# Two-stage attention and soft mixture of experts on one core: later stores in row halves on SyncE's queue, 28 zero products in front, one zero product fewer near the end

## The chip, the cores and the metric

The kernel runs on one core of a Trainium2 chip. The metric is device time in microseconds (us) for one launch. The core has a matrix engine (TensorE, in the profile PE, its weight loads PEld), a vector engine (VectorE, DVE), a scalar engine (ScalarE, ACT), a general engine (GpSimd, POOL) and a control engine (SyncE, SP). Transfers between the chip's memory (HBM) and the core's memory run on 16 DMA engines; they are issued here from POOL's queue and from SP's queue. Matrix products end in PSUM, from where DVE or ACT move them ("evict" them) to the core's main memory.

## The reference

There are two steps. The first is causal attention for 4 batches, 8 heads, 768 positions and head size 64; three of the heads see all earlier positions, the other five only the first 4 positions and a window of 64. The second is a soft mixture of experts on the 3072 rows of 512 that attention gives.

```python
scores = scale * np.matmul(q, k.transpose(0, 1, 3, 2))
scores = np.where(mask, scores, -1e9)          # causal; or causal & (first 4 | last 64)
a = softmax(scores); attn = np.matmul(a, v)    # -> x: (3072, 512)

logits = x @ phi                               # (3072, 32): 8 experts of 4 slots
d = softmax(logits, axis=0); slot_input = d.T @ x
for e in range(8):
    slot_out[e] = np.maximum(slot_input[e] @ w1[e], 0.0) @ w2[e]   # 512 -> 1024 -> 512
c = softmax(logits, axis=1)
out = c @ slot_out                             # (3072, 512) float32
```

## The kernel before

**Order of the work.** The kernel is written as a list of named steps, each with the engines that may do it, an assumed cost, a key (about the time at which it is due) and the steps and buffers that it needs. A planner in the file (`Plan.run`) simulates the engines and fixes one order per engine; that order is the program. Every engine then works through its own list and waits on semaphores for the others. The planner counts PE's instructions with the number `mm` that a step states, not with what its function emits.

**Attention.** A batch is worked in four pairs of heads. PE transposes the loaded rows of q, k and v (lines L604 for the first batch, L630 for the others, eviction by the helper lines L334 and L336), forms the scores (L656), ACT takes the exponential (L726), DVE multiplies by the mask (L672), PE multiplies by v (L800), DVE divides (L824), and PE transposes the result for the logits (L836).

**The front.** POOL issues the loads of the first batch and writes small index tables; the last of these is `unit` (L419). SP issues three transfers (L475 to L477): half of the first expert matrix, the flags of the heads, and phi. DVE sets `zt`, a tile of zeros (L499). PE's first step is `TD` (two products, L427 and L428), which needs the tables; then come the transposes of phi (L528), the flag product (L513), a second group for phi (L536), and the transposes of the first batch (L604). Between these stand five zero products of 448 columns (`ZG`, L505), which the planner places and whose results nobody reads.

**The mixture of experts.** The expert matrices come in fp32 and are cast to bf16 on the way in, all from POOL's queue. Of w1 and w2 most come as one transfer of 1 MB (as written); the last two matrices of w2 (numbers 14 and 15, the tiles pt and qk) come in two column halves of 256, in the order 14 left, 15 left, 14 right, 15 right, so that the left half of `slot_out` is ready before the right half has landed. After the products with w1 (L1008) and w2 (L1046) ACT scales a half of `slot_out` (L1104).

**The output.** It is 24 tiles of 128 rows by 512 columns: six groups `gi` of four tiles `r`, where the four tiles of a group hold interleaved rows. Groups 0, 1 and 2 are made in two column halves: all twelve left halves as soon as the left half of `slot_out` is there, then all twelve right halves; groups 3, 4 and 5 are then made whole. One output product is L1121, its eviction with the division by the row sum L1131 (DVE) or L1129 (ACT), in turns. The stores (L1140) are:

- left, from POOL's queue: group 0 as tile 0 and tiles 1 to 3; group 1; group 2 (four transfers);
- right, from SP's queue: group 0 as tiles 0 and 1, tiles 2 and 3; group 1; group 2 (four transfers);
- whole groups 3, 4 and 5, from SP's queue (three transfers of 1 MB).

Three zero products of 448 columns (`ZT0`, `ZT1`, L1064) stand in PE's list ahead of the last w2 matrix of each column half:

```python
for c in range(2):
    for e in range(NE - NSPLIT, NE):
        w2_op(e, c, c + 1)
        if e == NE - 2:
            wait_zeros(f"ZT{c}", 3, kt + (29.5 + e if c else 22.5), w2o[c], c == 0)
```

The store step, which the change calls with other rows and another queue:

```python
def store(eng, m, gi, r0, r1, cs, key):
    def emit_st(o):
        dst = out[512 * gi:512 * (gi + 1), :].rearrange("(p r) d -> p r d", r=4)
        (nc.gpsimd if eng == "POOL" else nc.sync).dma_start(dst[:, r0:r1, cs], ot_view(gi)[:, r0:r1, cs])
```

Of the kernel before, what the change touches and what calls it, by code (L numbers as in the profile page):

```python
# [151 lines left out]
def pe(ns, n=1):  # L152
    occ = ns * n / 1000.0
    return {"PE": (occ, occ + 0.27)}
# [72 lines left out]
def kernel(  # L227
# [13 lines left out]
    nc = tc.nc  # L241
    P = 128
    B, H, S, D = q.shape
# [37 lines left out]
    zt = sb.tile([P, 448], BF16, name="zt")  # L281
# [16 lines left out]
    tq, krow, unit = xr[:, 0:256], xr[:, 256:384], xr[:, 384:640]  # L298
    jrow = xT.rearrange("p a c -> p (a c)")[:, 1536:1792].bitcast(F32)
    td = xT.rearrange("p a c -> p (a c)")[:, 640:1152].bitcast(F32)  # L300
    rne, frow = xr[:, 1792:1824].bitcast(F32), xr[:, 1824:1832]
# [4 lines left out]
    trb = [ps.tile([P, 512], F32, name=f"tr{i}") for i in range(2)]  # L306
    pvb = ps.tile([P, 2, 512], F32, name="pv")

    def tr_bf(s, n):
        return trb[s].bitcast(BF16)[:, 0:n]  # L310
# [10 lines left out]
    pl = Plan({"S8": 11, "QT": 2, "KT": 2, "VT": 1, "VB": 2, "VF": 3, "PT": 2, "PTX": 2, "XB": 2,  # L321
               "XT": 1, "SC": 2, "TR": 2, "PV": 1, "BK": 8})
# [6 lines left out]
    def on(eng, occ, late=0.18):  # L329
        return {eng: (occ, occ + late)}  # L330
# [50 lines left out]
    def w_mem(i):  # L381

        m = late_mem[i]() if i in late_mem else slots[wbuf[i].slot][:, :]
        return m.rearrange("p (h x) -> p h x", h=2)[:, :, 0:4 * KB]
# [37 lines left out]
    def head_const(o):  # L422
        nc.vector.tensor_scalar(ident, jrow, pc[:, 0:1], None, op0=ALU.is_equal)

    def emit_td(o):
        t = trb[tdb.slot][:, 0:256]
        nc.tensor.matmul(t, unit[:, 0:128], tq, start=True, stop=False)  # L427
        nc.tensor.matmul(t, krow, unit, start=False, stop=True)  # L428

    def key_pos(o):  # L430
        t = trb[tdb.slot][:, 0:256]
        nc.vector.tensor_scalar(pc[:, 2:3], t[:, 0:1], -float(n_sink), None, op0=ALU.is_gt)
        nc.vector.tensor_copy(td, t)
        nc.vector.scalar_tensor_tensor(edist[:, 0:256], td, -30000.0, td, op0=ALU.mult, op1=ALU.max)
        nc.vector.tensor_copy(edist[:, 256:768].rearrange("p (a c) -> p a c", a=2),
                              edist[:, 0:256].rearrange("p (o c) -> p o c", o=1).to_broadcast([P, 2, 256]))
# [11 lines left out]
    def head_flags(o, n):  # L448
        cp = nc.scalar.copy if o.eng == "ACT" else nc.gpsimd.tensor_copy
        for a, j0, j1 in ((1, 1, 4), (0, 0, 1)):  # L450
            cp(fmx[:, n, :, j0:j1, :].rearrange("p i j d -> p i (j d)"),
               thr[:, a, n::4].rearrange("p (i o) -> p i o", o=1).to_broadcast([P, 2, 66 * (j1 - j0)]))
# [54 lines left out]
    for x in range(5):  # L507
        o_z = pl.op(f"ZG{x}", pe(372), 60.0, deps=[o_z], lead=9.6 + 1.2 * x, emit=emit_zg, mode="full", mm=1)
    o_kp = pl.op("key_pos", on("DVE", 1.2), -79, deps=[o_td], rel=[tdb], emit=key_pos)
    flb = Buf("TR")  # L510
    o_fr = pl.op("flag row", on("DVE", 0.2), -10, deps=[o_sp], emit=flag_row)
    o_fp = pl.op("flag product", on("PE", 0.07, 0.27), -10, deps=[o_fr, o_tab], acq=[flb], mode="r32", mm=1,
                 emit=lambda o: nc.tensor.matmul(trb[flb.slot][:, 0:H], unit[:, 0:128], frow, start=True, stop=True))  # L513
    o_fl = pl.op("flags", on("DVE", 0.45), -10, deps=[o_fp, o_kp], rel=[flb], emit=flags)
    o_fm, o_hm = {}, {}
    for n in range(4):
        o_fm[n] = pl.op(f"fm{n}", on("ACT", 0.65) if n == 0 else on("POOL", 0.9), -8 if n == 0 else T * n - 3.5,
                        deps=[o_fl], emit=lambda o, n=n: head_flags(o, n))
# [15 lines left out]
    def phi_t2(o):  # L534
        for n in range(4):
# [8 lines left out]
                  emit=lambda o: nc.vector.tensor_copy(  # L544
                      phi4, tr_bf(pb2.slot, 4 * NS).rearrange("p (n r s) -> p n r s", n=4, r=1).to_broadcast(
                          [P, 4, 4, NS])))
# [3 lines left out]
    def load_tile(ti):  # L550

        tbuf[ti], tland[ti], p0 = Buf("S8"), [], 0
        for x, b, x0, x1 in TILES[ti]:
# [8 lines left out]
                  emit=lambda o, x=x: nc.gpsimd.tensor_copy(w_mem(0)[:, 0, KB * x:KB * (x + 1)],  # L562
                                                            w0f[:, KB * x:KB * (x + 1)])) for x in range(4)]
# [82 lines left out]
    def evs(x, b, n):  # L646
        return ev[x, 0, n // 2] if b == 0 else [e for x0, x1, e in ev[x, b] if x0 < 6 * n + 6 and x1 > 6 * n]
# [32 lines left out]
    for b in range(B):  # L680
        for n in range(4):
# [5 lines left out]
            def emit_v2(o, n=n, tr=tr):  # L687
                t = tr_bf(tr.slot, 768)
                for j in range(6):
# [3 lines left out]
                      emit=emit_v2, mode="full", mm=6)  # L693

            def emit_vb(o, b=b, n=n, tr=tr):
# [4 lines left out]
                           acq=[VBb[b]] if n == 0 else [], rel=[tr], emit=emit_vb)  # L700
            VFb[p] = Buf("VF")

            def emit_vf(o, b=b, n=n, p=p):
# [4 lines left out]
                           emit=emit_vf)  # L708

            PTb[b, n] = Buf("PT")  # L710
            for kk, g in enumerate(range(5)):
# [3 lines left out]
                def emit_qk(o, b=b, n=n, g=g, sc=sc):  # L715
                    parts, c = [], 0
                    for j, q0, nb in PGROUPS[g]:
# [5 lines left out]
                          acq=[sc], rel=[QTb[b], KTb[b]], emit=emit_qk, mode="r64", mm=2 * len(PGROUPS[g]))  # L723

                def emit_ex(o, b=b, n=n, g=g, sc=sc):
# [4 lines left out]
                                   acq=[PTb[b, n]] if kk == 0 else [], rel=[sc], emit=emit_ex)  # L730
                for m, gs in enumerate(MGROUPS):
                    if gs[-1] == g:
                        o_m = pl.op(f"MK.{p}.{m}", on("DVE", [0.605, 0.605, 0.335][m]), key + 0.3,
                                    deps=[expo[p, x] for x in gs] + [o_hm[n]], emit=mask_emit(b, n, m))
# [3 lines left out]
        for ns in ([(0, 1), (2, 3)] if b == 0 else [(0, 1, 2, 3)]):  # L738
            sc = Buf("SC")

            def emit_lx(o, b=b, sc=sc, ns=ns):
# [4 lines left out]
                      deps=list(dict.fromkeys(e for n in ns for x in "qk" for e in evs(x, b, n))),  # L746
                      acq=[sc], rel=[QTb[b], KTb[b]], emit=emit_lx, mode="r64", mm=2 * len(ns))

            def emit_ex2(o, b=b, sc=sc, ns=ns):
# [4 lines left out]
            e = pl.op(f"EXX.{b}.{ns[0]}", on("ACT", 0.12 + 0.213 * len(ns)), key - 1.0, deps=[a, PTXb[b].op],  # L754
                      acq=[PTXb[b]] if ns[0] == 0 else [], rel=[sc], emit=emit_ex2)

            def emit_mx(o, b=b, ns=ns):
# [4 lines left out]
            e = pl.op(f"MX.{b}.{ns[0]}", on("DVE", 0.07 + 0.134 * len(ns)), key + 0.3, deps=[e] + [o_hm[n] for n in ns],  # L762
                      emit=emit_mx)
# [5 lines left out]
    for b in range(B):  # L769
        for n in range(4):  # L770
# [9 lines left out]
            for i in iorder:  # L780
                deps, need = [v2e[p], vfo[p]] + [o_z][p:], set()
# [7 lines left out]
                def emit_pv(o, b=b, n=n, p=p, i=i, pv_at=pv_at):  # L789
                    pT = pTs[PTb[b, n].slot]  # L790
                    vb = vbs[VBb[b].slot]
                    for h in range(2):
                        bk, c = pv_at(h, i)
                        for j in range(i + 1):
# [3 lines left out]
                            else:  # L798
# [5 lines left out]
                             deps=list(dict.fromkeys(deps)) + ([last] if last else []),  # L804
                             acq=[PVb[p]] if i == 0 else [],
# [7 lines left out]
            for i0, i1 in halves:  # L813
                part = f"{p}" if i1 - i0 == 6 else f"{p}.{i0}"

                def emit_nm(o, i0=i0, i1=i1, b=b, n=n, p=p):
# [3 lines left out]
                    else:  # L820
# [8 lines left out]
                                 deps=[pvo[i1 - 1], XBb[b].op], acq=[XBb[b]] if n == 0 else [], rel=[PVb[p]],  # L829
                                 emit=emit_nm)  # L830

                def emit_xt(o, i0=i0, i1=i1, b=b, n=n, tr=tr):
                    t = tr_bf(tr.slot, 768)
                    xv = xbs[XBb[b].slot]
                    for i in range(i0, i1):
# [3 lines left out]
                          acq=[tr] if i0 == 0 else [], rel=[XBb[b]], emit=emit_xt, mode="full", mm=i1 - i0)  # L839

                def emit_xe(o, i0=i0, i1=i1, n=n, tr=tr):
# [4 lines left out]
                               acq=[XTb[b]] if n == 0 else [], rel=[tr], emit=emit_xe)  # L846
# [9 lines left out]
        if b < B - 1:  # L856
            es = []
            for c in range(2):
                lg = Buf("TR")

                def emit_ls(o, c=c, lg=lg):
                    for n in range(4):
# [4 lines left out]
                          acq=[lg], rel=[XTb[b]], emit=emit_ls, mode="full", mm=4)  # L867
# [8 lines left out]
            def emit_tt(o, te=te):  # L876
                for i in range(6):
# [5 lines left out]
                           emit=lambda o, te=te: copy(o, elg.rearrange("p i s -> p (i s)"), tr_bf(te.slot, 6 * NS)))  # L883
# [8 lines left out]
        else:  # L892
            lg = Buf("TR")
            a = pl.op(f"LGa.{b}", pe(25, 18), kb - 6.0, deps=[xto[4 * b + n] for n in range(3)] + [o_phi],
                      acq=[lg], emit=lambda o, lg=lg, f=emit_lg: f(o, lg, ns=(0, 1, 2)), mode="full", mm=18)
            for i0 in (0, 3):
                a = pl.op(f"LG.{b}" if i0 else f"LGb.{b}", pe(25, 3), kb - 6.0, deps=[a, xhalf[i0]], rel=[XTb[b]],
                          emit=lambda o, lg=lg, f=emit_lg, i0=i0: f(o, lg, ns=(3,), i0=i0, i1=i0 + 3), mode="full", mm=3)
# [74 lines left out]
    kt = T * 16 + 10  # L973
# [7 lines left out]
    def emit_si(o):  # L981
        t = trb[si.slot][:, 0:4 * NS].rearrange("p (a s) -> p a s", a=4)
        sv = slot_sc.rearrange("p (di do) -> p do di", do=4)
        for do in range(4):
# [4 lines left out]
                  emit=lambda o: nc.vector.tensor_copy(siT.rearrange("p a s -> p (a s)"), trb[si.slot][:, 0:4 * NS]))  # L989
    zs, zb = [], Buf("SC")  # L990
    named = {o.name: o for o in pl.ops}
    for z, (name, n) in enumerate((("PV.15.5", 1), ("XT.15.3", 1), ("LG.3", 1), ("DS.3", 1), ("SI", 1))):
        def emit_z(o, n=n):
            for _ in range(n):
# [3 lines left out]
                        acq=[zb] if z == 0 else [], emit=emit_z, mode="full", mm=n))  # L998
    hse, hte = {}, {}
    for e4 in range(2):  # L1000
        hse[e4] = []
        for c in range(2):
            hp = Buf("BK")

            def emit_h(o, e4=e4, c=c, hp=hp):
                for do in range(4):
                    for g in range(4):
# [5 lines left out]
                      acq=[hp], emit=emit_h, mode="c32", mm=16)  # L1013
# [25 lines left out]
    w2o = {}  # L1039
# [21 lines left out]
    def wait_zeros(name, n, key, dep, first=False):  # L1061
        def emit_z(o):
            for _ in range(n):
                nc.tensor.matmul(banks[zw.slot][:, 0:448], ident, zt, start=True, stop=True)  # L1064

        pl.op(name, pe(190, n), key, deps=[dep], acq=[zw] if first else [], rel=[zw], emit=emit_z, mode="full", mm=n)
# [4 lines left out]
    for c in range(2):  # L1071
        for e in range(NE - NSPLIT, NE):
            w2_op(e, c, c + 1)
            if e == NE - 2:
                wait_zeros(f"ZT{c}", 3, kt + (29.5 + e if c else 22.5), w2o[c], c == 0)

    def out_lhs(gi, r):
        return expT[:, r, 128 * gi:128 * (gi + 1)]
# [2 lines left out]
    for x, (g0, g1) in enumerate(((0, 3), (3, 6))):  # L1081
# [8 lines left out]
        def emit_rr(o, g0=g0, g1=g1, rw=rw):  # L1090
# [4 lines left out]
                  acq=[rw], rel=[], emit=emit_rw, mode="full", mm=4 * (g1 - g0))  # L1095
# [4 lines left out]
    for c in range(2):  # L1100
        def emit_so(o, c=c):
# [3 lines left out]
            else:  # L1105
# [3 lines left out]
                          emit=emit_so))  # L1109
# [27 lines left out]
# [5 lines that stand above are left out]
        pl.op(f"ST.{m}.{gi}.{r0}", on(eng, 0.7), key, deps=[oe[m, gi, r] for r in range(r0, r1)], emit=emit_st)  # L1142

    NL = 12
    halved = [(gi, min(4, NL - 4 * gi)) for gi in range((NL + 3) // 4)]
    for gi, n in halved:
        for r in range(n):
            out_tile("l", gi, r, 0, 1, kt + 30 + 0.1 * (4 * gi + r))
    for gi, r0, r1 in [(0, 0, 1), (0, 1, 4)] + [(gi, 0, n) for gi, n in halved[1:]]:
        store("POOL", "l", gi, r0, r1, slice(0, 256), kt + 31 + gi + 0.1 * r0)  # L1150
    for gi, n in halved:
        for r in range(n):
            out_tile("r", gi, r, 1, 2, kt + 40 + 0.1 * (4 * gi + r))
        for r0, r1 in [(0, 2), (2, 4)] if gi == 0 else [(0, n)]:
            store("SP", "r", gi, r0, r1, slice(256, 512), kt + 41 + gi + 0.1 * r0)
    for gi in range(6):
        n = dict(halved).get(gi, 0)
# [55 lines left out]
```

## Time and profile before

| what | value |
|---|---|
| median of 3 runs | 148.62 us (148.15 to 148.8) |
| the profiled execution's own time | 148.91 us |
| its span, first to last instruction | 147.1 us |
| mean granted clock of TensorE | 0.968 |
| busy: PE, DVE, ACT, POOL | 119.7, 111.0, 107.9, 42.0 us |

The profile is of one execution on the chip. A row of the timeline gives the start and the length in us, the engine, the line of the kernel, the operation, what it writes and reads, its shape, how often it stands in that row, and in brackets the idle time before it and what ended that. A row of the chain of waits gives start, length and what the last chain of work was doing. The rows of transfers give their kind, their number, the size of each in KB, and the median time from issue to landing. "DMA share" is the mean busy share of the 16 DMA engines; it can exceed 1 where an engine has more than one packet under way.

### The profile page before, as it was taken

The page shows a single profiled execution, that of the slowest core. Times are in us where ns is not written, and L with a number is a line of the kernel's source. Part 1 is how long each engine was busy: PE and PEld are TensorE (multiplying, and loading weights), DVE is VectorE, ACT ScalarE, POOL GpSimd, SP SyncE. Part 2 cuts the span into 40 slices and gives each one's busy share as a digit, 9 for nine tenths or more (in the row PEclk, how much of TensorE's full clock was granted, in tenths as well). Part 3 has the DMA queues.
Part 4 walks back from the last instruction along what each step waited for, and adds up shares of the span by engine and source line. Part 5 has one row for each costly group of instructions (what it writes and reads, how often), then busy time and mean ns, then how long its engine had stood idle before and what let it go on. Part 6 is the DMA issues. An engine that isn't in the chain of part 4 may idle for free.

```text
span 147.1 us, 4879 instructions
## 1 busy us (share of the span) xinstructions
PE 119.7 (81%) x2107; PEld 79.2 (54%) x2107; DVE 111.0 (75%) x254; ACT 107.9 (73%) x147; POOL 42.0 (29%) x75
## 2 busy tenths in 40 slices
PE   0167988999989999999999999999959899879000
PEld 0045666677776657776558766666745445443000
DVE  1786299999999999999799899999973312549500
ACT  3152689999999997999998999999971460649200
POOL 6988631120311380100170011405380000340000
PEclk9999999999999999999999999999995999999965
DMA  5999999999999999999999999999999999989995
GB/s 147 270 207 212 217 213 214 213 215 211 216 215 214 212 215 214 217 214 214 215 215 217 214 215 214 214 214 215 214 214 214 206 196 197 168 309 347 404 423 212
DMA packets 13815, 33.40 MB, mean 227 GB/s; under 512 B 802, under 2 KB 6562, under 8 KB 13282
## 3 DMA queue, kind: packets, MB, share of 16 engines
q0 software_dynamic: 11472, 27.27, 94.1%
q1 hardware_dynamic: 2322, 5.83, 10.5%
q8 instruction: 16, 0.26, 0.6%
q14 instruction: 5, 0.04, 0.1%
HBM read 52.49 MB, written 6.29 MB: 400 GB/s over the span
## 4 chain that ended last, share of the span: by engine, by line
PE 27%; DVE 26%; DMA 18%; ACT 15%; issue 5%; POOL 1%; SPq 0%; DVEq 0%; ACTq 0%; POOLq 0%
DMA qk<-in_moe_w_dram 14%; ACT pt L726 11%; PE sc L656 6%; DVE pt L672 5%; PE pv L800 5%; DVE xv L824 5%; DMA phf<-in_moe_phi_dram 4%; DVE qk L336 4%; PE tr L604 3%; PE tr L630 3%; PE bk L1121 2%; PE tr L863 2%; DVE xv L336 2%; DVE slot L1131 2%; DVE vf L705 2%
## 5 line engine op out<-in xcount | busy, mean ns | idle before, releaser
L726 ACT ACTIVATE pt<-sc 128x1024 bf16<-128x1024 f32 x80 | 77.0, 1047 | 3.0 <-PE sc L656 2.8
L656 PE MATMUL sc<-qk 64*128 64x512 bf16 (+3 forms) x256 | 31.4, 311 | 1.2 <-ACT pt L726 0.8
L672 DVE TENSOR_TENSOR pt<-pt,msk 128x1024 bf16<-128x1024 bf16 (+1 forms) x48 | 29.0, 610 | 2.0 <-ACT pt L726 1.8
L800 PEld LDWEIGHTS <-pt 128*128 128x128 bf16 x640 | 23.4, 98 | 6.2 <-issue 5.2
L800 PE MATMUL pv<-vx,pt 128*128 128x65 bf16 x320 | 25.6, 193 | 0.3 <-DVE xv L824 0.2
L800 PE MATMUL pv<-vf,pt 128*128 128x65 bf16 x320 | 21.3, 195 | 0.9 <-DVE xv L824 0.9
L347 POOL DMA_DIRECT2D slot<-in_moe_w_dram x11 | 7.7, 696 | 40.0 <-PE tr L630 34.3
L336 DVE COPY qk<-tr 128x768 bf16<-128x768 bf16 (+2 forms) x33 | 15.1, 482 | 2.1 <-PE tr L604 1.8
L630 PE MATMUL tr<-ident,slot 128*64 128x128 bf16 (+1 forms) x448 | 16.3, 219 | 0.4 <-ACT qk L334 0.3
L824 DVE TENSOR_TENSOR xv<-pv,rs 128x768 bf16<-128x768 f32 (+1 forms) x17 | 15.5, 911 | 0.6
L630 PEld LDWEIGHTS <-slot 128*64 128x64 bf16 (+1 forms) x448 | 13.1, 109 | 5.1 <-issue 4.8
L656 PEld LDWEIGHTS <-qk 64*128 64x128 bf16 x256 | 10.4, 94 | 9.6 <-issue 3.3
L887 POOL COPY expT<-eT 128x192 bf16<-128x192 bf16 x12 | 7.4, 667 | 12.5 <-ACT eT L870 12.5
L1131 DVE TENSOR_SCALAR slot<-bk,rrow 128x256 f32<-128x256 f32 (+1 forms) x19 | 9.2, 562 | 2.2 <-PE bk L1121 2.2
L336 DVE COPY xv<-tr 128x512 bf16<-128x512 bf16 (+2 forms) x20 | 8.0, 410 | 2.5 <-PE tr L604 2.2
L836 PE MATMUL tr<-ident,xv 128*128 128x128 bf16 x96 | 8.4, 224 | 1.3 <-DVE xv L824 0.9
L604 PEld LDWEIGHTS <-slot 96*64 96x64 bf16 x192 | 6.8, 141 | 4.3 <-issue 4.0
L604 PE MATMUL tr<-ident_u,slot 96*64 96x96 bf16 x192 | 7.9, 248 | 1.6 <-DVE phi L544 1.1
L336 DVE COPY xT<-tr 128x768 bf16<-128x768 bf16 (+1 forms) x14 | 7.5, 539 | 1.1 <-PE tr L836 1.1
L1129 ACT ACTIVATE slot<-bk,rrow 128x256 f32<-128x256 f32 (+1 forms) x17 | 7.7, 570 | 0.9 <-PE bk L1121 0.9
L690 PE MATMUL tr<-ident,xv 128*128 128x128 bf16 x96 | 8.1, 220 | 0.0
L1140 POOL DMA_DIRECT2D out_dram<-slot x4 | 2.9, 714 | 17.7 <-DVE slot L1131 17.6
(121 smaller groups left out, 165.6 us busy)
## 6 DMA issues: line engine op xcount, KB each, us to landing
slot<-in_moe_w_dram POOLq DMA_DIRECT2D x10, 1024.0 KB, 24.6
out_dram<-slot SPq DMA_DIRECT2D x3, 1024.0 KB, 5.9
slot<-in_q_dram POOLq DMA_DIRECT2D x2, 768.0 KB, 19.9
slot<-in_k_dram POOLq DMA_DIRECT2D x2, 768.0 KB, 23.8
qk<-in_moe_w_dram SPq DMA_DIRECT2D x1, 1024.0 KB, 6.3
slot<-in_v_dram POOLq DMA_DIRECT2D x2, 512.0 KB, 21.5
qk<-in_moe_w_dram POOLq DMA_DIRECT2D x1, 1024.0 KB, 17.4
vx<-in_moe_w_dram POOLq DMA_DIRECT2D x1, 1024.0 KB, 21.5
```

Source lines behind the costliest of these rows:

```text
L336: nc.vector.tensor_copy(dst, src)
L347: acq=[buf] if buf else [], lead=1.3, emit=lambda o: nc.gpsimd.dma_start(dst(), src))
L604: nc.tensor.transpose(t[64 * i:64 * (i + 1), :, :, s, :], rv[:, i, 8 * c + s, :], ident_u)
L630: nc.tensor.transpose(t[64 * i:64 * (i + 1), :, s, :], rv[:, i, 8 * c + s, :], ident[0:R, 0:R])
L656: nc.tensor.matmul(scb[sc.slot][:, i, c:c + 128 * nb], kk, qq.rearrange("p b c -> p (b c)"), start=True, stop=True)
L672: nc.vector.tensor_tensor(pT, pT, mh, op=ALU.mult)
L690: nc.tensor.transpose(t[:, 128 * j:128 * (j + 1)], vT[:, 6 * n + j, :], ident)
L726: nc.scalar.activation(pTs[PTb[b, n].slot][:, :, 512 * g:512 * (g + 1)], scb[sc.slot], ACT.Exp, scale=scale)
L800: nc.tensor.matmul(pvb[:, bk, c:c + 65], lt, rhs, start=(j == 0), stop=(j == i))
L824: nc.vector.tensor_tensor(xo, pvw[:, :, :, 0:64], r.rearrange("p i (j o) -> p i j o", o=1).to_broadcast([P, 2, i1 - i0, 64]), op=ALU.mult)
L836: nc.tensor.transpose(t[:, 128 * i:128 * (i + 1)], xv[:, i, 128 * n:128 * (n + 1)], ident)
L1131: nc.vector.tensor_scalar(d, banks[bf.slot][:, 0:w], sc_, None, op0=ALU.mult)
```

## The change

Three edits.

1. In front, 28 zero products of 256 columns enter PE's list: 15 ahead of TD, 10 behind it, 3 behind the flag product. They write a part of PSUM that nobody reads before it is written anew. The planner's counts are not changed, so all other steps keep their order on every engine.
2. `ZT1`, ahead of the last w2 matrix of the right half, has two zero products instead of three.
3. The left stores of groups 1 and 2 go from POOL's queue to SP's, each in two transfers (tiles 0 and 1, tiles 2 and 3); on SP's queue they stand ahead of the right stores. The right stores of groups 1 and 2 are split in the same way. With the three transfers of the front, SP's queue then carries sixteen.

```diff
+    def fill(n):
+        for _ in range(n):
+            nc.tensor.matmul(pvb[:, 1, 0:256], zt[:, 0:128], zt[:, 0:256], start=True, stop=True)
+
     def emit_td(o):
+        fill(15)
         t = trb[tdb.slot][:, 0:256]
         nc.tensor.matmul(t, unit[:, 0:128], tq, start=True, stop=False)
         nc.tensor.matmul(t, krow, unit, start=False, stop=True)
+        fill(10)
...
-    o_fp = pl.op("flag product", on("PE", 0.07, 0.27), -10, deps=[o_fr, o_tab], acq=[flb], mode="r32", mm=1,
-                 emit=lambda o: nc.tensor.matmul(trb[flb.slot][:, 0:H], unit[:, 0:128], frow, start=True, stop=True))
+    def emit_fp(o):
+        nc.tensor.matmul(trb[flb.slot][:, 0:H], unit[:, 0:128], frow, start=True, stop=True)
+        fill(3)
+
+    o_fp = pl.op("flag product", on("PE", 0.07, 0.27), -10, deps=[o_fr, o_tab], acq=[flb], mode="r32", mm=1, emit=emit_fp)
...
-                wait_zeros(f"ZT{c}", 3, kt + (29.5 + e if c else 22.5), w2o[c], c == 0)
+                wait_zeros(f"ZT{c}", 2 if c else 3, kt + (29.5 + e if c else 22.5), w2o[c], c == 0)
...
-    for gi, r0, r1 in [(0, 0, 1), (0, 1, 4)] + [(gi, 0, n) for gi, n in halved[1:]]:
-        store("POOL", "l", gi, r0, r1, slice(0, 256), kt + 31 + gi + 0.1 * r0)
+    for gi, r0, r1 in [(0, 0, 1), (0, 1, 4)] + [(gi, x, x + 2) for gi, n in halved[1:] for x in (0, 2)]:
+        store("SP" if gi else "POOL", "l", gi, r0, r1, slice(0, 256), kt + 31 + gi + 0.1 * r0)
...
-        for r0, r1 in [(0, 2), (2, 4)] if gi == 0 else [(0, n)]:
+        for r0, r1 in [(0, 2), (2, 4)]:
             store("SP", "r", gi, r0, r1, slice(256, 512), kt + 41 + gi + 0.1 * r0)
```

## The prediction

> **What bounds the kernel now.** I read the page first, then the chain of waits, then the timeline of the last 20 us and the busy shares by stretch, and last the timeline of the first 16 us.
>
> ```profile
> span 147.1 us, 4879 instructions
> ...
> DMA  5999999999999999999999999999999999989995
> ...
> q8 instruction: 16, 0.26, 0.6%
> ...
> HBM read 52.49 MB, written 6.29 MB: 400 GB/s over the span
> ```
>
> The DMA engines are full in nearly every slice. What they carry is seen by stretch (columns: stretch, length, busy time of PE, PEld, DVE, ACT, POOL, granted clock, DMA share, GB/s):
>
> ```profile
> 0.00:1.70 1.70, 0.00 (x0) 0.00 (x0) 0.24 (x1) 0.97 (x1) 0.57 (x5) 1.00 0.00 0
> 1.70:2.70 1.00, 0.00 (x0) 0.00 (x0) 0.00 (x0) 0.31 (x1) 1.00 (x2) 1.00 0.95 205
> 30.00:105.00 75.00, 73.09 (x1407) 50.99 (x1404) 71.95 (x156) 72.39 (x92) 17.50 (x27) 1.00 1.06 214
> 110.00:115.00 5.00, 4.52 (x67) 2.92 (x66) 1.31 (x4) 1.35 (x3) 0.00 (x0) 0.66 1.05 211
> 127.00:131.00 4.00, 3.03 (x38) 1.41 (x37) 2.07 (x7) 2.41 (x7) 2.85 (x4) 1.00 0.79 203
> 132.00:145.00 13.00, 3.91 (x18) 1.44 (x15) 6.21 (x12) 4.94 (x11) 0.00 (x0) 0.85 1.03 397
> 134.00:137.00 3.00, 1.94 (x8) 0.58 (x6) 3.00 (x6) 2.94 (x6) 0.00 (x0) 1.00 1.05 368
> 137.00:145.00 8.00, 0.00 (x0) 0.00 (x0) 1.21 (x2) 0.00 (x0) 0.00 (x0) 0.75 1.03 422
> 145.00:147.10 2.10, 0.00 (x0) 0.00 (x0) 0.00 (x0) 0.00 (x0) 0.00 (x0) 0.50 0.10 39
> ```
>
> Two stretches are full: the loads (share 1.06 at 30 to 105 us) and the stores (1.03 at 132 to 145). Between them, at 127 to 131, the share falls to 0.79. The chain and the issue-to-landing table say what hangs on that seam:
>
> ```profile
> 107.20 0.09 POOL qk L347
> ...
> 108.94 21.16 DMA qk<-in_moe_w_dram
> 130.15 0.43 PE bk L1046 x8
> 130.59 0.48 ACT msk L1104
> ```
>
> ```profile
> qk<-in_moe_w_dram POOLq DMA_DIRECT2D x2, 512.0 KB, 19.4
> ...
> out_dram<-slot SPq DMA_DIRECT2D x2, 256.0 KB, 2.8
> ```
>
> The last half of the last w2 matrix (w15, in qk) is issued at 108.94 and lands at 130.1, because 21 us of other loads are queued ahead of it. From its landing everything right of column 256 follows in a row:
>
> ```profile
> 125.31 0.40 PE L1046 MATMUL bk<-qk,xT 128*32 128x256 bf16 x8
> ...
> 126.59 2.44 DVE L1131 TENSOR_SCALAR slot<-bk,rrow 128x256 f32<-128x256 f32 x6 [1.96 <-PE bk L1121]
> 126.70 2.30 ACT L1129 ACTIVATE slot<-bk,rrow 128x256 f32<-128x256 f32 x6 [0.47 <-PE bk L1121]
> ...
> 127.37 2.96 POOL L1140 DMA_DIRECT2D out_dram<-slot  x4 [17.56 <-DVE slot L1131]
> ...
> 128.56 0.74 PE L1064 MATMUL bk<-zt,ident 128*128 128x448 bf16 x3
> ...
> 130.15 0.40 PE L1046 MATMUL bk<-qk,xT 128*32 128x256 bf16 x8 [0.84 <-DMA qk<-in_moe_w_dram]
> ...
> 132.09 0.97 SPq L1140 DMA_DIRECT2D out_dram<-slot  x2
> ```
>
> PE idles 0.84 us for that load at 130.15; the first right-hand store leaves SP at 132.09, 1.94 us after the landing. So the time is: landing (130.15), 1.94 us of compute, and then stores at the full rate until 145.2. After 132.0 the engines move 13.0 x 397 + 2.1 x 39 KB = 5.24 MB of the 6.29 MB of output. The right halves (12 tiles of 128x256 f32, 1.57 MB) and the twelve full tiles (3.15 MB) make 4.72 MB, so 0.52 MB of left-hand output is still unsent when the right-hand stores begin. At the 368 GB/s of 134 to 137, where the runs are 1 KB, that is 1.4 us: the left stores end at about 133.4.
>
> **The zero products in front.** These rows carry their cost:
>
> ```profile
> 0.85 0.24 DVE L499 MEMSET zt<- 128x224 uint32 x1 [0.85 <-PEq L1194]
> ...
> 4.55 0.39 PE L427 MATMUL tr<-xT 1*128 1x256 bf16 x1 [4.55 <-POOL xT L419]
> 4.73 0.42 PE L428 MATMUL tr<-xT 1*128 1x256 bf16 x1
> ...
> 8.01 0.61 PE L528 MATMUL tr<-ident,phi 128*32 128x128 bf16 x4 [2.86 <-DVE xT L439]
> 8.55 0.18 PE L513 MATMUL tr<-xT 1*128 1x8 bf16 x1
> 9.28 0.28 PE L536 MATMUL tr<-ident,slot_acc 32*128 32x32 bf16 x4 [0.55 <-ACT slot_acc L334]
> ...
> 11.92 1.49 PE L604 MATMUL tr<-ident_u,slot 96*64 96x96 bf16 x32 [1.09 <-DVE phi L544]
> 13.34 0.93 PE L505 MATMUL pv<-zt 128*128 128x448 bf16 x2
> 14.20 1.49 PE L604 MATMUL tr<-ident_u,slot 96*64 96x96 bf16 x32
> 15.62 0.55 PE L505 MATMUL pv<-zt 128*128 128x448 bf16 x1
> ...
> 115.04 0.35 PE L995 MATMUL sc<-zt,ident 128*128 128x448 bf16 x1
> ```
>
> Two zero products of 448 columns take 0.93 us at 13.34 and one takes 0.55, so each further one costs 0.38. At the end three take 0.74 and one 0.35: 0.195 each. PE is at half speed in front, although the clock column shows 1.00 there. Scaled to 256 columns, a product costs 0.22 us in front and 0.11 at full speed. The first fifteen can start when zt is set (1.09) and end at 1.1 + 15 x 0.22 = 4.4 us; PE waits for POOL until 4.55 anyway, so they cost nothing (if zt came 0.5 us later, TD would be 0.35 us late). The ten behind TD run from 5.15 to 7.35 at most and PE waits for DVE until 8.01: nothing. The three behind the flag product run from 8.73 to 9.06 or 9.39, and the next product waits for ACT until 9.28: 0 to 0.1 us.
>
> What they bring is clock. The four groups at 11.92, 13.34, 14.20 and 15.62 alone are 4.46 us at half speed, so up to 2.2 us leave PE's front; since PE alternates there with landings and evictions I put the earlier start of attention at 1 to 1.5 us. The Trainium skill's "TensorE: Matmul & The Clock Gate", section "Part 1: The HAM clock gate", has full clock after a busy window of about 3.4 us and half clock after an idle one; the halved prices of the zero products agree, and by it the fillers release the clock before the transposes.
>
> Where does that 1 to 1.5 us go? Attention is engine-bound (PE, DVE, ACT 96 to 97% busy at 30 to 105 us), so it ends that much earlier. But the load that gates the right half is not: the DMA share is already 1.06 throughout and the last load is 21 us deep in its queue. I count 0 on the end. Only the left half can start sooner: its product at 125.31 needs the other qk half, issued at 107.20. The median of the two is 19.4 and one took 21.2, so the other took 17.6 and landed at 124.8: 0.5 us sooner at most.
>
> The 28 products add 56 instructions (weight load and product) to PE's stream and so move the points at which its code is fetched; the page has 16 such fetches of 16 KB. The trace shows no price for a late one. I bound it by 0 and by the 1 to 1.5 us gained plus the 0.84 us idle, which cover it, and take 0.
>
> **One zero product fewer before the last half.** It saves 0.2 us at 128.56 to 129.3, where PE then waits 0.84 us: 0 gain. If that cover were gone, 0.2 us gain. PE's idle time before 130.15 grows to about 1.1 us, or 1.6 with the left half sooner; in a stretch with long waits the clock column fell to 0.66 (110 to 115). If that came at 130, the eight products (0.40) and the first output product would take some 0.35 us longer: 0 to +0.35, I take 0, since only the last of these idles exceeds a microsecond.
>
> **The stores.** POOL loses two transfers; SP goes from seven to thirteen. A store's issue on SP is short:
>
> ```profile
> L1140 SPq DMA_DIRECT2D out_dram<-slot x7: 332/408/621, 132.1 to 138.3; - x7
> ```
>
> Six right-hand issues at 0.41 to 0.62 us from 132.09 end at 134.6 to 135.8, while the engines are busy with earlier ones: no cost. In the built program SP's sixteen transfers share eight completion semaphores, so each of the last five stores waits for a store eight places earlier; the tightest, the last (138.3 now), waits for the first right-hand one, issued at 132.09 and landed 2.8 us later: no cost. On SP the four new left stores stand ahead of the right ones, but their tiles are done by 129.1: no cost.
>
> The gain is in when they flow. DVE and ACT finish a pair of tiles every 0.41 us, so rows 0 and 1 of the second group are ready at 127.9, the others at 128.3, 128.7 and 129.1. SP's first issue of the kernel, at 0.73 us, moves its first byte at about 1.7 (no byte before 1.7, 205 GB/s after), 1.0 us later. So the SP stores flow from 129.0, into a stretch that is 0.79 full. All 1.57 MB at 368 GB/s take 4.3 us; from 128.4 on (POOL's first store at 127.37 plus the same 1.0) that ends at 132.7 instead of 133.4. The right-hand stores cannot flow before 132.09 + 1.0 = 133.1. So they move from 133.4 to 133.1: **0.3 us saved**. The lower bound is 0 (the left stores still end at 133.4, since 1 KB runs move at 368 GB/s against 422 for the long ones). The upper bound is the unfilled time, (1.03 - 0.79) x 4 = 0.96 us.
>
> **Sum.** Against the profiled execution's own time of 148.91 us (span 147.1 and 1.8 around it): 0 + 0 + 0 - 0.3 = 148.6. It lies 0.3 above the median of 148.62, so on the median's scale 148.3. A difference of 0.5%, 0.74 us, is about the least that a measurement of this kernel can tell from no change.
>
> **Rivals.** *The left stores delay the last load (slower).* Before, all left stores stood behind the load in POOL's own queue; now two thirds come on SP's queue from 129.0 (128.5 if the left half starts sooner) and can take turns with a load that lands at 130.15. At equal turns for the 1.1 to 1.6 us of overlap, the load lands 0.5 to 1.6 us later. That decides from 0.3 us on: the right half then starts later than the left stores end, the engines run dry, and the end moves by the delay less 0.3. That is +0.2 to +1.3; I take +0.9, 149.5 us. For it: the load is the chain's only gate. Against it: in the trace the right-hand stores' first landing (132.09 + 2.8 = 134.9) comes after the left ones are out, and the share falls before 131, so most engines have finished the load.
>
> The Trainium skill's "DMA: Bandwidth & Descriptors", section "Queues, rings and completion order", states this rule: each engine goes round the queues that have work, a whole packet at a time. No stretch of this trace has SP stores beside POOL loads to show it.
>
> *The warm front reaches the end (faster).* If issues that wait for PE's transposes were what spaced the loads, they would all land 1 to 1.5 us sooner: 147.4 us. Against it: share 1.06 and a 21 us queue. For it: PE, DVE and ACT are as full as the DMA engines, so a little slack in the loads would show.
>
> **How the numbers follow.** Forecast 0.60 (0.55 within 0.5%, 0.05 faster by its upper bound); the delayed load 0.25 (0.20 beyond +0.5%, 0.05 within); the warm front through to the end 0.15. So faster 0.20, same 0.60, slower 0.20. The range takes in the upper bound of the forecast and most of both rivals: 147.3 to 149.8. The likeliest case alone is 147.7 to 148.7.
>
> **What would show it.** Right: zero products end before 4.6 us; the 32 transposes now at 11.92 take about 0.75 us; PE's wait for qk grows to 1 us or more and its end stays within 0.2 us of 130.15; the share at 129 to 131 rises to about 1; the first right-hand store still leaves at 132.1. Wrong: qk lands after 130.5 (delayed load), or before 129.7 (warm front), or the 13 us of stores shrink by more than 0.5 us.

## The result and the profile after

| | before | after |
|---|---|---|
| median, six runs each | 148.4 us (147.86 to 148.87) | 147.44 us (147.35 to 147.56) |
| ratio after to before | | 0.9936, 95% interval 0.9915 to 0.9956 |
| profiled execution, its span | 148.91, 147.1 us | 147.56, 145.8 us |

The changed kernel is faster, by 0.44 to 0.85%. In two later series it was faster by 0.56 and 0.65 us (e5 and e12 below), so 0.6 us is the better single figure. The lines are read in the order of the prediction. First the page of the changed kernel:

```profile
span 145.8 us, 4941 instructions
...
PEclk9985699999999999999999999999995999999965
DMA  5999999999999999999999999999999999999995
...
q8 instruction: 16, 0.26, 0.6%
...
HBM read 52.49 MB, written 6.29 MB: 403 GB/s over the span
```

The DMA row no longer has the 8 near its end. The PEclk row (granted clock in tenths, 3.6 us a digit) starts at 9, falls to 5 and 6 and is back at 9 from about 17 us on. The 9 at its start says nothing yet: the first record of the clock in this trace is its rise at 6.69 us, and the first fifteen products ran at half speed (3.38 us, 0.225 each). The fills woke the clock, but it did not stay. By stretch (columns as before):

```profile
127.00:131.00 4.00, 2.85 (x40) 1.55 (x40) 1.93 (x6) 2.02 (x6) 1.11 (x2) 1.00 1.02 292
129.00:131.00 2.00, 1.35 (x26) 1.01 (x26) 0.49 (x2) 0.62 (x2) 0.00 (x0) 1.00 0.99 362
132.00:145.00 13.00, 3.23 (x13) 1.06 (x11) 5.53 (x11) 4.25 (x9) 0.00 (x0) 0.80 0.98 380
```

The seam at 127 to 131 is filled: 1.02 and 292 GB/s, against 0.79 and 203. Now the timeline, front and end, and SP's stores by their source line (the last row of products on qk is the right half of the last w2 matrix; its start is taken as the landing of its load):

```profile
1.15 3.38 PE L427 MATMUL pv<-zt 128*128 128x256 bf16 x15 [1.15 <-DVE zt L505]
...
5.00 2.07 PE L427 MATMUL pv<-zt 128*128 128x256 bf16 x10
...
8.11 0.50 PE L427 MATMUL pv<-zt 128*128 128x256 bf16 x3
...
8.85 0.53 PE L613 MATMUL tr<-ident_u,slot 96*64 96x96 bf16 x16
...
11.10 1.49 PE L613 MATMUL tr<-ident_u,slot 96*64 96x96 bf16 x32 [1.43 <-DVE phi L553]
...
13.38 1.49 PE L613 MATMUL tr<-ident_u,slot 96*64 96x96 bf16 x32
...
127.35 10.62 SPq L1149 DMA_DIRECT2D out_dram<-slot  x13
...
127.97 0.55 PE L1073 MATMUL bk<-zt,ident 128*128 128x448 bf16 x2
...
129.46 0.40 PE L1055 MATMUL bk<-qk,xT 128*32 128x256 bf16 x8 [0.95 <-DMA qk<-in_moe_w_dram]
```

```profile
L1149 SPq DMA_DIRECT2D out_dram<-slot x13: 344/447/662, 127.3 to 137.6; - x13
```

The first fifteen fills end at 4.53, before the 4.6 of the forecast. The 16 transposes at 8.85 run at full speed (0.53 us against 0.85 for the same 16 in the profile of before), the next 32 again take 1.49. The last half matrix lands at 129.46, 0.69 us earlier than in the profile of before. After that come the stores, and then a part that the prediction had quoted as a row (145.0 to 147.1, share 0.10) and not worked out: what SP does once the last byte is out. Two views of before: stretches, and SP's end-of-program semaphore waits (their line is L1208; count, shortest, median and longest in ns, first and last start):

```profile
145.00:145.50 0.50, 0.00 (x0) 0.00 (x0) 0.00 (x0) 0.00 (x0) 0.00 (x0) 0.50 0.41 164
145.50:146.30 0.80, 0.00 (x0) 0.00 (x0) 0.00 (x0) 0.00 (x0) 0.00 (x0) 0.50 0.00 0
```

```profile
L1208 SPq EVENT_SEMAPHORE  x7: 28/28/28, 145.8 to 146.2; - x7
L1208 SPq DRAIN  x1: 7/7/7, 146.3 to 146.3; - x1
```

The same two views of after (the line is now L1217):

```profile
144.00:144.50 0.50, 0.00 (x0) 0.00 (x0) 0.00 (x0) 0.00 (x0) 0.00 (x0) 0.50 0.40 164
144.50:145.00 0.50, 0.00 (x0) 0.00 (x0) 0.00 (x0) 0.00 (x0) 0.00 (x0) 0.50 0.00 0
```

```profile
L1217 SPq EVENT_SEMAPHORE  x1: 28/28/28, 144.9 to 144.9; - x1
L1217 SPq DRAIN  x1: 7/7/7, 145.0 to 145.0; - x1
```

Before, SP still goes through seven waits after the last byte, 0.06 us apart (145.84 to 146.20); after, through one. SP waits for its eight completion semaphores in a fixed order. Its transfers take them in turn, so the place of the last store decides how many waits come behind it: before it was SP's tenth transfer and used the second semaphore; now it is the sixteenth and uses the eighth. The six waits behind that of the last store were for transfers long landed, but each takes its 0.06 us.

The packets in the trace put the last byte of the stores at 145.48 before and at 144.52 after. With that the 1.35 us between the two profiled executions come apart into four terms:

| term | before | after | difference |
|---|---|---|---|
| landing of the last load | 130.15 | 129.46 | -0.69 |
| landing to last byte stored | 15.33 | 15.06 | -0.27 |
| last byte to the end of the span | 1.62 | 1.26 | -0.36 |
| outside the span | 1.81 | 1.78 | -0.03 |

Which of them belong to the change, the experiments had to tell.

### The profile page after: what moved, and what is told of

Its sections match the earlier page's. It is cut to its first block, busy times and chain, and to the rows that moved or that the text cites. A ratio compares the mean times of both kernels' runs of the same rounds, so it can differ in the third digit from the quotient of the medians.

```text
span 145.8 us, 4941 instructions
## 1 busy us (share of the span) xinstructions
PE 124.6 (85%) x2134; PEld 82.3 (56%) x2134; DVE 110.8 (76%) x254; ACT 107.9 (74%) x147; POOL 40.5 (28%) x73
## 4 chain that ended last, share of the span: by engine, by line
PE 28%; DVE 25%; DMA 18%; ACT 15%; issue 6%; POOL 1%; SPq 0%; DVEq 0%; ACTq 0%; POOLq 0%
DMA qk<-in_moe_w_dram 15%; ACT pt L735 11%; PE sc L665 6%; DVE pt L681 5%; PE pv L809 5%; DVE xv L833 5%; DMA phf<-in_moe_phi_dram 4%; DVE qk L336 3%; PE tr L613 3%; PE tr L639 3%; PE bk L1130 3%; PE tr L872 2%; DVE slot L1140 2%; DVE vf L714 2%; PE tr L845 2%
## 5 line engine op out<-in xcount | busy, mean ns | idle before, releaser
L613 PE MATMUL tr<-ident_u,slot 96*64 96x96 bf16 x192 | 7.3, 238 | 1.9 <-DVE phi L553 1.4
L613 PEld LDWEIGHTS <-slot 96*64 96x64 bf16 x192 | 6.3, 133 | 4.5 <-issue 4.1
L845 PEld LDWEIGHTS <-xv 128*128 128x128 bf16 x96 | 6.0, 99 | 2.9 <-DVE xv L833 1.7
```

The source lines that it names most:

```text
L613: nc.tensor.transpose(t[64 * i:64 * (i + 1), :, :, s, :], rv[:, i, 8 * c + s, :], ident_u)
L845: nc.tensor.transpose(t[:, 128 * i:128 * (i + 1)], xv[:, i, 128 * n:128 * (n + 1)], ident)
```

## Experiments

Each kernel was timed in twelve runs (e12 in eleven) beside the kernel before on the same chip; e1 to e4, e5 to e8 and e9 to e12 are one series each, with the kernel before at 148.36, 148.16 and 148.35 us.

**e1: the fills alone.** Only the 28 products (the diff's `fill` lines) are added to the kernel before.

> Only the 28 zero products in front; stores and ZT1 as before. Theory A (the stores bring 0.3 us, the products bring the rest by an earlier landing of the last load): 0.5 to 0.7 us faster than before, last load landing 0.5 to 0.7 us earlier than in the profile of before (130.15), stores as before. Theory B (all 0.96 us comes from the stores): within 0.1 us of before. Theory C (the earlier landing is a difference between two executions): within 0.1 us in the median, landing anywhere between 129.4 and 130.2.

148.35 us, ratio 0.999 (0.9964 to 1.0017): no difference that the interval can tell from none. The end of its timeline, its seam, and SP's last waits:

```profile
129.63 0.40 PE L1055 MATMUL bk<-qk,xT 128*32 128x256 bf16 x8 [1.03 <-DMA qk<-in_moe_w_dram]
...
131.57 0.95 SPq L1149 DMA_DIRECT2D out_dram<-slot  x2
```

```profile
127.00:131.00 4.00, 2.77 (x39) 1.41 (x38) 1.66 (x6) 1.78 (x5) 2.52 (x4) 1.00 0.96 275
```

```profile
L1217 SPq EVENT_SEMAPHORE  x7: 28/28/28, 145.2 to 145.6; - x7
```

**e2: the stores alone.** Only edit 3 of the change.

> Only the stores: left groups 1 and 2 on SP, row halves; no products in front, ZT1 as before. Theory A: 0.3 us faster, landing of the last load as before. Theory B: 0.9 us faster. Theory C: 0.3 us or more, with the landing anywhere between 129.4 and 130.2.

147.75 us, ratio 0.9949 (0.9923 to 0.9975): 0.61 us faster. Its profile has the tail of the whole change: 15.06 us from landing to last byte, one wait behind it.

```profile
L1208 SPq EVENT_SEMAPHORE  x1: 28/28/28, 144.9 to 144.9; - x1
```

**e3: one zero product fewer, alone.**

```diff
-                wait_zeros(f"ZT{c}", 3, ...
+                wait_zeros(f"ZT{c}", 2 if c else 3, ...
```

> Only ZT1 with two zero products instead of three. All theories: within 0.1 us of before, PE's wait for the last load about 0.2 us longer (1.05 instead of 0.84).

148.25 us, ratio 0.9987 (0.9956 to 1.0018): again no difference clear of the interval.

**e4: the kernel before, unchanged.**

> The kernel before, unchanged, once more, for the spread of the landing of the last load from one execution to the next. Theories A and B: landing within 0.2 us of 130.15. Theory C: it differs by some tenths, and the time with it.

148.24 us, ratio 0.9991 (0.9963 to 1.0019). Its profiled execution is the one that settles the landing:

```profile
129.30 0.40 PE L1046 MATMUL bk<-qk,xT 128*32 128x256 bf16 x8 [0.55 <-DMA qk<-in_moe_w_dram]
...
131.24 1.40 SPq L1140 DMA_DIRECT2D out_dram<-slot  x2
```

```profile
127.00:131.00 4.00, 3.25 (x42) 1.85 (x42) 2.14 (x7) 2.24 (x6) 2.66 (x4) 1.00 0.91 258
```

The same program landed its last load at 129.30 here and at 130.15 in the first profile; its seam was 0.91 full, not 0.79. So the 0.69 us of the first comparison can't be credited to the change. Nor did the early landing bring time: this execution took 148.55 us, because its first right store, issued at 131.24, moved its first byte only at 132.92 (by the packets), when the left stores on POOL's queue were nearly out (133.34), and its landing to last byte is 15.83.

**e5: the changed kernel again.**

> The changed kernel once more, so that the three beside it are compared with it in one and the same series of runs. Every theory: about 147.45 us, 0.9 below the kernel before. The stretch from the landing of the last load to the last byte stored, 15.06 us in its first profile, should be near that again even if the landing itself differs by some tenths; if the landing comes at 130.1 here and the time stays at 147.5, the shorter stretch isn't what counts.

147.6 us, ratio 0.9957 (0.9934 to 0.998). By chance this profile holds the test of the warm front. Its clock row and its front:

```profile
PEclk9999999999999999999999999999999999689955
```

```profile
10.84 0.87 PE L613 MATMUL tr<-ident_u,slot 96*64 96x96 bf16 x32 [1.24 <-DVE phi L553]
...
12.26 0.87 PE L613 MATMUL tr<-ident_u,slot 96*64 96x96 bf16 x32
...
124.08 0.40 PE L1055 MATMUL bk<-qk,xT 128*32 128x256 bf16 x8 [1.58 <-DMA qk<-in_moe_w_dram]
...
127.03 5.74 SPq L1149 DMA_DIRECT2D out_dram<-slot  x7
...
129.38 0.40 PE L1055 MATMUL bk<-qk,xT 128*32 128x256 bf16 x8 [0.56 <-DMA qk<-in_moe_w_dram]
```

Here the clock stayed full from 5.5 us to the end of attention and beyond, the transposes took 0.87, and attention's last product with v came at 107.52 instead of 110.16. The landing was 129.38 and the time 147.49, against 129.46 and 147.56 without. So 2.6 us won in front bring nothing at the end. They only move PE's long wait: it now waits 1.58 us for the left half of the last matrix, and the dip near the end of the clock row is half clock from 124.92 to 128.34, over before the landing.

**e6: the change without its fills.**

> The changed kernel without its 28 products in front: stores on SyncE's queue and two products of zeros behind the left half. Theory 1 (all of the gain is the stores'): 147.45, the same as the changed kernel beside it within 0.2. Theory 2 (the fills add 0.3 once the stores no longer hide it; the stores alone gave 147.75 and the whole change 147.44, in different series): 147.75, 0.3 above the changed kernel.

147.54 us, ratio 0.9966 (0.9939 to 0.9994). Theory 1 holds: no part of the gain that these runs can measure is the fills'.

**e7 and e11: whole-group stores on SP's queue.** Left and right stores of groups 1 and 2 are one transfer each again; the left ones stay on SP.

```diff
-    for gi, r0, r1 in [(0, 0, 1), (0, 1, 4)] + [(gi, x, x + 2) for gi, n in halved[1:] for x in (0, 2)]:
+    for gi, r0, r1 in [(0, 0, 1), (0, 1, 4)] + [(gi, 0, n) for gi, n in halved[1:]]:
         store("SP" if gi else "POOL", "l", gi, r0, r1, ...
-        for r0, r1 in [(0, 2), (2, 4)]:
+        for r0, r1 in [(0, 2), (2, 4)] if gi == 0 else [(0, n)]:
```

> The changed kernel with the stores of groups 1 and 2 as whole groups again, left ones on SyncE's queue: tells the queue from the size. Theory 1 (the end is the draining of the left stores, and SyncE's queue lets them leave sooner and beside GpSimd's): most of the gain stays, 147.5 to 147.8. Theory 3 (the halves count: bytes leave as soon as two rows are evicted instead of four): little is left, 148.1 to 148.4, as the kernel before.

147.98 us, ratio 0.9987 (0.9958 to 1.0015), 0.38 above e5. Seam and last waits of e7:

```profile
127.00:131.00 4.00, 3.39 (x41) 1.74 (x40) 1.54 (x5) 1.76 (x5) 0.43 (x1) 0.78 1.05 315
```

```profile
L1217 SPq EVENT_SEMAPHORE  x5: 28/28/28, 144.5 to 144.7; - x5
```

The transfers are as good as the change's (share 1.05, landing to last byte 15.05), yet the time isn't. I repeated it.

> The kernel with whole-group stores on SyncE's queue once more: it gave 147.98 by its median though its profiled execution took 147.40 and kept the transfers as busy as the changed kernel (share 1.07 in the seven microseconds about the landing, against 1.06). Theory 1 (only the queue counts; the median was the landing's scatter): within 0.15 of the changed kernel beside it. Theory 3 (the halves count too): again 0.3 to 0.4 above it.

148.13 us, 0.43 above e12; landing to last byte 15.05. The first median, 147.98, lies between the ranges of Theory 1 (up to 147.8) and Theory 3 (from 148.1); the second, 0.43 above the change, is near what Theory 3 said. But its reason (halves count) doesn't show in the profiled executions: the bytes leave as early. What differs is SP's count: twelve transfers put the last store on the fourth semaphore, five waits where the change has one, 4 x 0.06 = 0.24 us (last byte to end 1.50 against 1.26). The other 0.14 and 0.19 us lie within the intervals. They have the same sign in e8 below (0.15), though, so it stays open whether something else costs there.

**e8: row halves, all left stores on POOL's queue.**

```diff
-        store("SP" if gi else "POOL", "l", gi, r0, r1, ...
+        store("POOL", "l", gi, r0, r1, ...
```

> The changed kernel with its left stores, in row halves, all on GpSimd's queue: six issues there, 0.75 us apart in the kernel before, so that the last would leave at about 126.8 + 5 x 0.75 = 130.5, 1.5 us later than the last left store of the kernel before (129.04). Theory 1 (the queue counts): no gain, 148.3 to 149.0, the last left bytes drain at 133.5 or later and hold the right ones. Theory 3 (the halves count): near the changed kernel, 147.4 to 147.8.

147.99 us, ratio 0.9982 (0.9961 to 1.0003). Its last left store was issued at 129.75, earlier than the 130.5 reckoned, and its landing to last byte is 15.11: in this one execution SP's queue wasn't needed for that term either. Its SP queue also has twelve transfers and five waits, 1.50 us after the last byte. So of the 0.39 us that it lies above e5, 0.24 are waits again. With 147.99 it lies between the ranges of both theories.

**e9: the change without the left stores of group 2.**

```diff
-        store("SP" if gi else "POOL", "l", gi, r0, r1, ...
+        if gi < 2:
+            store("SP" if gi else "POOL", "l", gi, r0, r1, ...
```

> The changed kernel with the left stores of group 2 left out (those 0.52 MB of the output are never written). Tells whether the end is the total of the bytes or a path through the landing of the last load. Theory 1 (from the left stores to the end the transfers are never idle, so every byte counts, also those that go out beside the load): 0.52 MB less at 423 GB/s, the rate of the last stretch, is 1.24 us, at the 363 GB/s of the half rows 1.44: 146.2 to 146.4. Theory 4 (the left stores run in gaps beside the load, and the end is the landing plus the right path): no change, 147.5. Between them lies the case that a gap of some tenths opens in front of the right stores: 146.5 to 147.0.

147.44 us, 0.26 below e12, although two transfers fewer on SP's queue leave three waits and cost 0.12 (1.38 from last byte to end against 1.26): the bytes themselves brought some 0.38. Theory 1 (every byte counts) falls, Theory 4 nearly holds:

```profile
127.00:131.00 4.00, 3.18 (x35) 1.17 (x33) 1.14 (x4) 1.42 (x4) 0.68 (x1) 0.50 1.01 293
131.00:131.50 0.50, 0.50 (x4) 0.30 (x3) 0.40 (x1) 0.18 (x1) 0.00 (x0) 0.50 0.30 105
131.50:133.00 1.50, 1.50 (x9) 1.03 (x8) 1.48 (x5) 1.33 (x4) 0.00 (x0) 0.50 0.16 57
133.00:134.00 1.00, 1.00 (x4) 0.44 (x3) 1.00 (x3) 0.83 (x3) 0.00 (x0) 0.50 1.03 339
```

The bytes left out open a hole of (1 - 0.30) x 0.5 + (1 - 0.16) x 1.5 = 1.6 us in front of the right stores; 0.42 of it is this execution's half clock (the 0.50 in the rows), with which the first right store left 2.35 us after the landing instead of 1.93 (this is a warm front too: the half clock began at 125.95, after PE had waited 1.57 us for the left half). The other 1.2 us are about the time of the 0.52 MB. In the change, then, the left stores are out about when the right ones begin to flow; there is little more to gain from moving them, some 0.4 us at most by this run.

**e10: two groups in column halves instead of three.** `NL = 8` instead of 12.

> The changed kernel with two groups stored in column halves instead of three (groups 2 to 5 as whole rows). Half rows left at about 363 GB/s (four microseconds from 130 on, 351 to 374), whole rows at 423, so 1.05 MB moved from one to the other saves 2.89 - 2.48 = 0.41 us; but 0.52 MB less is ready before the right half lands, 1.44 us of cover. Theory 1 (no idle time is left and only the rate counts, if the cover holds): 147.1. Rival (the left bytes run out before the right ones flow at about 132.3): up to 1.0 of idle against 0.4 saved, 147.6 to 148.1. I lean to the rival.

148.57 us, ratio 1.0027 (1.0004 to 1.005), 0.87 above e12. The rival won, by more than I gave it:

```profile
131.50:133.00 1.50, 1.50 (x7) 0.75 (x6) 1.50 (x4) 1.17 (x4) 0.00 (x0) 0.50 0.26 85
```

Landing to last byte grew by 1.10 (16.16), of which 0.2 are this execution's half clock (its first right store left 2.13 us after the landing instead of 1.93), and thirteen transfers leave four waits, 0.18 us more.

**e12: the changed kernel, beside e9 to e11.**

> The changed kernel, for the three beside it in the same series: 147.5 to 147.6 by every theory, the kernel before 148.2 to 148.4.

147.7 us, ratio 0.9954 (0.9935 to 0.9974). In its profiled execution (148.29 us) PE waited longer for the load, and then worked at half speed (timeline, then stretches):

```profile
130.05 0.62 PE L1055 MATMUL bk<-qk,xT 128*32 128x256 bf16 x8 [1.57 <-DMA qk<-in_moe_w_dram]
```

```profile
131.00:132.00 1.00, 0.84 (x8) 0.57 (x5) 0.58 (x2) 0.33 (x2) 0.00 (x0) 0.50 1.06 372
132.00:133.00 1.00, 1.00 (x7) 0.68 (x5) 0.99 (x4) 0.83 (x3) 0.00 (x0) 0.50 0.63 216
```

Its first right store left 2.35 us after the landing instead of 1.93, a hole opened, and landing to last byte was 15.20 instead of 15.06.

**All profiled executions together** (us; "waits" counts those from the last store's own on; "last byte" is by the packets of the trace):

| kernel | time | landing | landing to last byte | SP transfers | waits | last byte to end |
|---|---|---|---|---|---|---|
| before | 148.91 | 130.15 | 15.33 | 10 | 7 | 1.62 |
| e4 before | 148.55 | 129.30 | 15.83 | 10 | 7 | 1.63 |
| e1 fills | 148.26 | 129.63 | 15.21 | 10 | 7 | 1.63 |
| e3 one zero fewer | 147.83 | 129.13 | 15.27 | 10 | 7 | 1.62 |
| e7 whole on SP | 147.40 | 129.07 | 15.05 | 12 | 5 | 1.50 |
| e11 the same | 148.19 | 129.87 | 15.05 | 12 | 5 | 1.50 |
| e8 halves on POOL | 147.97 | 129.58 | 15.11 | 12 | 5 | 1.50 |
| e10 two halved | 149.00 | 129.59 | 16.16 | 13 | 4 | 1.45 |
| e9 no left stores of group 2 | 147.98 | 129.50 | 15.22 | 14 | 3 | 1.38 |
| e2 stores | 147.55 | 129.44 | 15.06 | 16 | 1 | 1.27 |
| e6 no fills | 147.25 | 129.11 | 15.09 | 16 | 1 | 1.25 |
| after | 147.56 | 129.46 | 15.06 | 16 | 1 | 1.26 |
| e5 after | 147.49 | 129.38 | 15.06 | 16 | 1 | 1.27 |
| e12 after | 148.29 | 130.05 | 15.20 | 16 | 1 | 1.27 |

The last column follows the count of SP's transfers in every row, 0.06 us for each wait. Landing to last byte is 15.41 on the mean of the four executions with the old stores and 15.09 on that of the five with the new ones; without the 15.83 of e4 the difference is 0.18 instead of 0.32. The landing scatters over 1.1 us, and neither the stores, nor the fills, nor a front at full clock (e5, e7, e9, e11: 129.07 to 129.87) orders it. So the change is worth 0.32 + 0.36 = 0.68 us in these executions, beside 0.56 to 0.65 measured by the medians of e2, e5, e6 and e12. The 0.96 of the first comparison is above this; the scatter of the landing, a few tenths on medians of six, would make up the rest, but no run shows it for those.

## Why the prediction was right, and where it was wrong

The measured 147.44 lies in the range, at its lower end, and that was luck in part: the range went down to 147.3 for the unfilled share of the seam (0.96 us) and for the warm front (147.4 us), and the runs bear out neither. The forecast of 148.3 was too high by 0.9, and "faster by over 0.5%" had only 0.2. Of the 0.9, 0.2 are the median of before, 148.40 in six runs instead of 148.62 in three, and 0.7 the gain, 0.96 here instead of 0.3; beside the 0.6 of the later series the sum lacks the 0.36 of the waits behind the last store.

**Right: the fills.** They hide where the prediction said, and bring nothing on the end that e1 and e6 can tell from 0. The reason given, that the last load doesn't ask when attention ends, was shown by e5, whose attention ended 2.6 us earlier. The rival of the warm front is refuted with it. What the prediction didn't see is a risk: with a warm front PE's long wait falls ahead of the left half (1.57 to 1.79 us in e5, e7, e9 and e11), half clock came with it each time, and in e9 it outlasted the landing and made the right path 0.42 us longer.

**Wrong on the way: the clock.** The 32 transposes were to take 0.75 us; they took 1.49 in the profile after and 0.87 in e5. Of the nine profiled executions with fills, four kept the full clock, five lost it again at 9.7 to 11.2 us. The Trainium skill's "TensorE: Matmul & The Clock Gate", section "Part 1: The HAM clock gate", says that the activity window runs freely and isn't tied to the kernel's start; executions of one program that differ, as after and e5, agree with that. The prediction took from that section of the Trainium skill only that the fillers would release the clock. The gain in front was mis-sized too: with the clock kept, attention ended 2.6 us earlier (e5), not 1 to 1.5; in the profile after its last product with v came at 110.16, against 110.06 to 110.72 in the executions without fills.

**Right: the zero product, with its danger.** No effect of edit 2 shows (e3). The bound of +0.35 us, should the clock fall in the longer wait, was real in e12: the wait was 1.57 us and the right path 0.42 longer. With waits up to 1.10 us (e3) the clock held. No execution had a wait between the two, so whether the third zero product would have kept the clock in e12 isn't shown.

**Right: the stores' transfers.** The prediction counted 0.3 us, from left stores that end before the right ones can flow; 0.32 was measured as the mean, 0.27 in the pair of first profiles, and 0.18 without e4, so the near match is partly luck. The mechanism shows in the packets: the first right byte moved 1.23 to 1.68 us after its issue with the old stores (in before at 133.51, where the prediction had 133.4), and 0.89 us after it in e9, where the left stores were out by then. The share at 129 to 131 is 0.99 as it should be. The upper bound of 0.96, the unfilled share of the seam, wasn't a measure of anything: e4, e1 and e3 had 0.91, 0.96 and 0.99 there with the same stores, and their landing to last byte was 15.83, 15.21 and 15.27, against 15.33 at 0.79.

**Refuted: the rival of the delayed load.** With left stores on SP's queue from about 127 on, the landing stayed within the scatter of the kernel before (129.11 to 130.05 against 129.13 to 130.15).

**Missing: the waits behind the last store.** The prediction looked at the shared semaphores ("SP's sixteen transfers share eight completion semaphores") only for what they cost while stores are issued, and took the 1.8 us and the last row of the stretches as fixed. That step lacked -0.36 us, more than half of the gain of 0.6. It could have been counted blind: ten transfers and sixteen, eight semaphores, and seven waits in the trace of before behind the last byte.

**Wrong: the landing as a fixed point.** "Its end stays within 0.2 us of 130.15" failed (129.46), and with it "the first right-hand store still leaves at 132.1" (131.39). By the prediction's own sign, a landing before 129.7 was to mean the warm front; e4, with no change at all, landed at 129.30. One profile can't say how far a time that is set by a deep queue of loads moves between executions.

## What to carry to other kernels

Count what stands between the last byte and the end of the program: which of the completion semaphores the last transfer uses sets how many waits follow it, and adding or removing transfers moves that. Before a time in one profile is used as a fixed point, and before a shift of some tenths in it is credited to an edit, profile the unchanged kernel a second time. Stores that fill the time until the last results are ready are worth moving only until they end as those begin; leaving out 0.52 MB there (e9) opened a hole of 1.2 us and brought some 0.4.

## What the runs showed of the hardware

- A wait for a semaphore that was satisfied long ago still costs SP 0.06 us (seven from 145.84 to 146.20), at the end of the program, where nothing covers it.
- The landing of a load 21 us deep in its queue moved between 129.07 and 130.15 us in fourteen executions, and between 129.30 and 130.15 in two of one and the same program (before, e4).
- In seven of the fourteen executions PE waited 1.57 to 1.79 us for a half of the last matrix (the left in e5, e7, e9, e11, the right in e8, e10, e12). Half clock began in each of them, between the last 0.2 us of that wait and 1.8 us after it. In the other seven these waits were at most 1.10 us, and the clock stayed full from 115 to 138 us.
